# A depthwise conv on VectorE feeding a two-layer MLP on TensorE: taps issued across the chunks in turn, and four blocks in halves instead of nine

## Chip, cores, metric

One core of one Trainium2 chip. The metric is the time of one execution on the device in microseconds (us), the median of several runs. A profile is one execution of its own; its span is some 1.7 us shorter than the time.

## The reference, cut to what matters

```python
# x [8, 4096, 192], weight [8 heads, 7 taps]; softmax over the taps, then a causal conv per channel
out = np.einsum('hk,bskhg->bshg', softmax(weight), x_unfolded)
# 32768 tokens: 192 -> 2048 -> 192
h = x @ w_in
g = np.maximum(0.01 * h, h)
return g @ w_out
```

## The kernel before

A block is 512 positions of two batch rows, 32 blocks in all. Three chunks of 64 channels lie beside one another in a block's conv tile `y`; the two batch rows share the 128 partitions. VectorE does the conv of the next block while TensorE does the two layers of this one. The first nine blocks go in two halves of 256 positions, each a "group" of its own:

```python
NHALF = 9
groups = [(b, h * HT, HT) for b in range(NHALF) for h in range(2)]
groups += [(b, 0, ST) for b in range(NHALF, NBLK)]

def conv_jobs(grp, chunks=range(NCH)):            # NCH = 3 chunks, K = 7 taps
    ...
    for c in chunks:
        for k in range(K):
            ...
            if k == 0:
                jobs.append(... nc.vector.tensor_scalar_mul(d, s, wk[:, c, 0:1]))
            else:                                  # d = s * wk + d
                jobs.append(... nc.vector.scalar_tensor_tensor(
                    out=d, in0=s, scalar=wk[:, c, k:k+1], in1=d, op0=mult, op1=add))
```

A step of TensorE is a part of the first layer (`mm1`: 12 matmuls of 512 columns, or 24 of 256 in a half; on 64 rows each) and then 16 slots of the second layer (`mm2`: 32 matmuls of 192 columns). A whole block has eight steps, a half four. A whole block's second layer can only begin when its first is complete, so at the passage from halves to whole blocks a plan cuts the second layer short for a while:

```python
plan = {
    2 * NHALF - 2: [16, 8, 8, 16],
    2 * NHALF - 1: [8, 8, 16, 16],
    2 * NHALF: [16, 8, 8, 16, 8, 8, 16, 16],
}
...
copy = nc.scalar.copy if b < NHALF else nc.vector.tensor_copy     # eviction of the second layer
```

Of the kernel before, what the change touches and what calls it, by code (L numbers as in the profile page):

```python
# [14 lines left out]
def kernel(  # L15
# [11 lines left out]
    H, K = weight.shape  # L27
# [13 lines left out]
    NFC = F // 128  # L41
    NB = S // ST
    NBLK = (B // 2) * NB
    NHALF = 9
    RUN = 4
    NPEC = 2

# [14 lines left out]

    groups = [(b, h * HT, HT) for b in range(NHALF) for h in range(2)]
    groups += [(b, 0, ST) for b in range(NHALF, NBLK)]

# [107 lines left out]
    def conv_jobs(grp, chunks=range(NCH)):  # L173
        blk, t0, T = grp
        rp, st = divmod(blk, NB)
        if blk not in yt:
            yt[blk] = yt_pool.tile([128, NCH, ST], BF16, name="yt")
        y = yt[blk]
        jobs = []
        for c in chunks:  # L180
            for k in range(K):
                a = BASE + k + st * ST + t0
                src = xt[rp][:, c, a : a + T]
                dst = y[:, c, t0 : t0 + T]
                if k == 0:
                    jobs.append(
                        lambda s=src, d=dst, c=c: nc.vector.tensor_scalar_mul(  # L187
                            d, s, wk[:, c, 0:1]
                        )
                    )  # L190
                else:
                    jobs.append(
                        lambda s=src, d=dst, c=c, k=k: nc.vector.scalar_tensor_tensor(  # L193
                            out=d, in0=s, scalar=wk[:, c, k : k + 1], in1=d,
                            op0=mybir.AluOpType.mult, op1=mybir.AluOpType.add,
                        )
                    )
        return jobs
# [176 lines left out]
    for job in conv_jobs(groups[0], range(NPEC, NCH)):  # L375
        job()
# [92 lines left out]
    def evac_o(n):  # L469
# [4 lines left out]
        o_sb = osb[n // 2]  # L474
        copy = nc.scalar.copy if b < NHALF else nc.vector.tensor_copy
        ins = copy(out=o_sb[:, n % 2, :], in_=po.pop(n))  # L476
# [16 lines left out]
# [5 lines that stand above are left out]
    slot, avail = 0, 0  # L498
    for i, grp in enumerate(groups):
# [6 lines left out]
        if i == 0:  # L506
            ahead = []
        else:
            ahead = conv_jobs(groups[i + 1]) if i + 1 < len(groups) else []
        per = -(-len(ahead) // steps)  # L510
        for j in range(steps):
            for u in range(2 * j, 2 * j + 2):
                mm1(grp, u)
                if i == 0 and u == 1:
                    transpose_first(1)
                    evac_first(1, nc.vector.tensor_copy, nc.vector.tensor_copy)
                    pe_ahead, evac_y = pe_conv_jobs(groups[1], 0)
                    ahead = conv_jobs(groups[1], range(1, NCH))
                    per = len(ahead)
                if i == 0 and u == 3:  # L520

                    for job in pe_ahead:
                        job()
                    evac_y(act_scale)
                if i == 0 and u == 6:
                    transpose_first(2)
# [64 lines left out]
```

## Time and profile before

| | before |
|---|---|
| time, median of 3 runs | 692.91 us (692.07 to 692.96) |
| TensorE busy, profile | 684.0 of 690.9 us |
| VectorE busy, profile | 550.1 us |
| period of a step, halves / whole blocks | 2.630 / 2.615 us |

The prediction shows and reads the lines of this profile. One pair more is VectorE's accumulating taps by shape. Columns: line, engine, operation, names, shapes, count | busy us, mean ns of one | idle us before.

```profile
L193 DVE SCALAR_TENSOR_TENSOR yt<-xt,wk,yt 128x512 bf16<-128x512 bf16 x414 | 310.0, 749 | 10.2
L193 DVE SCALAR_TENSOR_TENSOR yt<-xt,wk,yt 128x256 bf16<-128x256 bf16 x306 | 148.4, 485 | 10.9
```

Busy time is 749 and 485 ns times the count: within a row nothing overlaps, and small gaps add up to 10 us in each.

### The profile page before, as it was taken

The numbers are of one execution on the slowest core, as the hardware profiler recorded it, in microseconds if no ns is written. First come the engines' busy times: TensorE is split into PE (matmuls) and PEld (weight loads), VectorE is DVE, ScalarE is ACT, GpSimd is POOL, SyncE is SP. The second block draws the span as 40 slices with busy tenths as digits, with TensorE's granted clock in tenths as the row PEclk, the third lists the DMA queues.
The fourth block names the chain that finished last, engine by engine and source line by source line (L and its number), as shares of the span: only waits on it lengthen the run. The fifth ranks groups of instructions, "written<-read, shape, count | busy, mean of one in ns | idle before, by whom it ended". The sixth has DMA issues, their size and how long they took to land.

```text
span 690.9 us, 26980 instructions
## 1 busy us (share of the span) xinstructions
PE 684.0 (99%) x12188; PEld 599.2 (87%) x12188; DVE 550.1 (80%) x1051; ACT 527.0 (76%) x609; POOL 147.1 (21%) x206
## 2 busy tenths in 40 slices
PE   8999999999999999999999999999999999999998
PEld 6999999999988888888888888888888888888887
DVE  6999999999986787878787878877878878787812
ACT  6888888888898777777777777777777777777771
POOL 7822220222222202222102222102222112000000
PEclk9999999999999999999999999999999999999999
DMA  9976454556649445566445565445664455322112
GB/s 153 117 92 94 76 79 82 68 75 83 82 71 94 72 81 74 67 93 82 67 84 68 75 83 87 74 74 76 77 82 74 81 73 70 67 60 59 47 42 65
DMA packets 184163, 53.85 MB, mean 78 GB/s; under 512 B 149104, under 2 KB 183664, under 8 KB 184048
## 3 DMA queue, kind: packets, MB, share of 16 engines
q0 software_dynamic: 99536, 14.76, 30.2%
q1 hardware_dynamic: 84512, 37.38, 22.8%
q8 instruction: 95, 1.56, 1.0%
q14 instruction: 20, 0.16, 0.1%
HBM read 29.88 MB, written 25.17 MB: 80 GB/s over the span
## 4 chain that ended last, share of the span: by engine, by line
PE 96%; ACT 1%; DMA 1%; POOL 1%; issue 0%; DVE 0%; POOLq 0%
PE po L429 49%; PE ph L403 47%; ACT g L410 1%; DMA w_in<-in_moe_w_in_dram 1%; POOL w_in L249 0%; POOL x_rows L123 0%; POOL sel L234 0%; DVE o_sb L476 0%; PE ptr L156 0%; POOL ident masks.py:199 0%; POOL sel L232 0%; POOL ident masks.py:197 0%; PE ptr L149 0%; POOLq masks.py:199 0%; POOLq L575 0%
## 5 line engine op out<-in xcount | busy, mean ns | idle before, releaser
L410 ACT ACTIVATE g<-ph 128x1024 bf16<-128x1024 f32 x512 | 496.2, 1021 | 143.2 <-PE ph L403 142.7
L193 DVE SCALAR_TENSOR_TENSOR yt<-xt,wk,yt 128x512 bf16<-128x512 bf16 (+1 forms) x720 | 458.3, 637 | 21.1
L429 PE MATMUL po<-w_out,g 64*128 64x192 bf16 (+1 forms) x8064 | 387.7, 243 | 0.0
L403 PE MATMUL ph<-yt,w_in 64*128 64x512 bf16 (+1 forms) x3936 | 384.7, 329 | 1.3 <-ACT g L410 0.7
L429 PEld LDWEIGHTS <-g 64*128 64x128 bf16 (+1 forms) x8064 | 360.5, 94 | 28.8 <-issue 0.2
L403 PEld LDWEIGHTS <-w_in 64*128 64x128 bf16 x3936 | 245.0, 111 | 54.6 <-issue 3.5
L78 POOL DMA_DIRECT2D x_bf<-in_x_dram x180 | 133.7, 777 | 424.6 <-DMA xt<-x_bf 422.0
L476 DVE COPY o_sb<-po 128x192 f32<-128x192 f32 x184 | 65.6, 357 | 109.1 <-PE po L429 100.4
L187 DVE TENSOR_SCALAR yt<-xt,wk 128x512 bf16<-128x512 bf16 (+1 forms) x120 | 40.6, 338 | 1.7 <-DMA xt<-x_bf 1.5
L476 ACT COPY o_sb<-po 128x192 f32<-128x192 f32 x72 | 23.0, 319 | 3.9 <-PE po L429 0.2
L284 PE MATMUL warm<-zero 128*128 128x256 bf16 (+1 forms) x20 | 4.5, 384 | 1.1 <-DVE junk L229 1.1
L212 PE MATMUL acc<-xt,diag 64*64 64x256 bf16 x84 | 5.0, 269 | 0.2 <-ACT xt L168 0.2
L168 DVE COPY xt<-ptr 128x384 bf16<-128x384 bf16 x7 | 2.2, 351 | 3.6 <-PE ptr L156 3.6
L212 PEld LDWEIGHTS <-diag 64*64 64x64 bf16 x84 | 4.5, 106 | 0.6 <-DVE xt L168 0.3
L127 POOL DMA_DIRECT2D x_half<-in_x_dram x6 | 4.3, 717 | 3.0 <-DMA w_in<-in_moe_w_in_dram 3.0
L284 PEld LDWEIGHTS <-zero 128*128 128x128 bf16 x20 | 2.4, 132 | 2.0 <-DVE junk L229 1.1
L249 POOL DMA_DIRECT2D w_in<-in_moe_w_in_dram x6 | 3.9, 656 | 0.0
L345 ACT ACTIVATE diag<-ident,whm 128x64 bf16<-128x64 bf16 x14 | 3.5, 335 | 0.0
L123 POOL DMA_DIRECT2D x_rows<-in_x_dram x4 | 2.9, 736 | 0.0
L156 PE MATMUL ptr<-ident,x_rows 64*64 64x64 bf16 x48 | 1.0, 196 | 1.3 <-DMA x_rows<-in_x_dram 1.3
L156 PEld LDWEIGHTS <-x_rows 64*64 64x64 bf16 x48 | 0.6, 108 | 1.9 <-DMA x_rows<-in_x_dram 1.7
L371 ACT ACTIVATE yt<-acc,rsum 128x256 bf16<-128x256 f32 x3 | 1.4, 467 | 1.0 <-PE acc L212 1.0
(37 smaller groups left out, 12.6 us busy)
## 6 DMA issues: line engine op xcount, KB each, us to landing
out_dram<-o_sb SPq DMA_DIRECT2D x117, 192.0 KB, 2.1
x_bf<-in_x_dram POOLq DMA_DIRECT2D x180, 64.0 KB, 3.3
out_dram<-o_sb SPq DMA_DIRECT2D x22, 96.0 KB, 1.6
xt<-x_bf SPq DMA_TRANSPOSE x90, 2.5
w_in<-in_moe_w_in_dram POOLq DMA_DIRECT2D x4, 192.0 KB, 5.6
w_in<-in_moe_w_in_dram POOLq DMA_DIRECT2D x2, 384.0 KB, 9.1
w_out<-in_moe_w_out_dram POOLq DMA_DIRECT2D x1, 768.0 KB, 11.2
x_nat<-in_x_dram SPq DMA_DIRECT2D x2, 192.0 KB, 2.6
```

The lines of the kernel that those rows point to most:

```text
L78: nc.gpsimd.dma_start(out=t[:, c, :, e, :], in_=src[2 * rp + e, :, :, c * CH : (c + 1) * CH],)
L127: nc.gpsimd.dma_start(out=x_half[q][:, c, :, e, :], in_=rows[:, e, :, c * CH : (c + 1) * CH],)
L187: lambda s=src, d=dst, c=c: nc.vector.tensor_scalar_mul(d, s, wk[:, c, 0:1])
L193: lambda s=src, d=dst, c=c, k=k: nc.vector.scalar_tensor_tensor(out=d, in0=s, scalar=wk[:, c, k : k + 1], in1=d, op0=mybir.AluOpType.mult, ...
L212: lambda k=k, p=p, a=a, e=e, ps=ps: nc.tensor.matmul(out=acc[ps, :T], lhsT=diag[c][ps, p, k, :], rhs=xt[0][ps, c, a : a + T], start=(k == ...
L249: nc.gpsimd.dma_start(out=w_in[n][e * CH : (e + 1) * CH], in_=moe_w_in[:, fs].rearrange("(c p) f -> p c f", p=CH),)
L284: nc.tensor.matmul(out=wa[:, 0, 0:cols], lhsT=zero[:, 0:128], rhs=zero[:, 0:cols], start=True, stop=True,)
L345: nc.scalar.activation(out=diag[c][:, p, k, :], in_=ident2, func=mybir.ActivationFunctionType.Copy, scale=whm[:, c, p, k : k + 1],)
L403: nc.tensor.matmul(out=ph[:, e, i * T : (i + 1) * T], lhsT=w_in_of(f, ps, c), rhs=y[ps, c, t0 : t0 + T], start=(c == 0), stop=(c == NCH - 1),)
L410: act = nc.scalar.activation(out=g[blk][:, nf * u : nf * (u + 1), :, t0 : t0 + T], in_=ph.rearrange("p e (i t) -> p i e t", i=nf), func=my ...
L429: return nc.tensor.matmul(out=po[m], lhsT=g[b][ps, fc, e, s * 128 : (s + 1) * 128], rhs=w_out[ps, fc, :], start=start, stop=stop,)
L476: ins = copy(out=o_sb[:, n % 2, :], in_=po.pop(n))
```

## The change

Each tap reads the accumulator that the tap before it wrote; such taps start 0.52 us apart in a half in the profile before, 35 ns more than one takes. Going through the chunks in turn, three accumulators alternate, and a tap need not wait for its neighbour: in the same profile, where a chunk ends, the next one's first tap starts 83 ns before the last tap's end. With a faster conv, fewer blocks should need to go in halves, and whole blocks need half the first-layer instructions.

```diff
-    NHALF = 9
+    NHALF = 4
...
-        for c in chunks:
-            for k in range(K):
+        for k in range(K):
+            for c in chunks:
```

## The prediction

> **What bounds the kernel now.** I read the page first: busy time by engine, the 40 slices, the chain that ended last, the waits; then the timeline of TensorE in one stretch with half blocks and one with whole blocks; last the timeline of VectorE.
>
> ```profile
> span 690.9 us, 26980 instructions
> PE 684.0 (99%) x12188; PEld 599.2 (87%) x12188; DVE 550.1 (80%) x1051; ACT 527.0 (76%) x609; POOL 147.1 (21%) x206
> PE   8999999999999999999999999999999999999998
> DVE  6999999999986787878787878877878878787812
> PE 96%; ACT 1%; DMA 1%; POOL 1%; issue 0%; DVE 0%; POOLq 0%
> ```
>
> TensorE is busy 684 of 690.9 us and is 96% of the chain that ended last. The listed waits of its matmuls come to 1.3+1.1+0.7+0.3+0.2 = 3.6 us, all in the start-up (input data, ScalarE's results), and none is for a conv result of VectorE. VectorE is close to full only in the first 12 slices or so, the nine blocks that go in halves.
>
> A busy TensorE may still not be at its peak, so I took the period of a step (the first-layer matmuls and then 32 second-layer ones):
>
> ```profile
> 102.88 1.51 PE L403 MATMUL ph<-yt,w_in 64*128 64x256 bf16 x24
> 104.19 1.52 PE L429 MATMUL po<-w_out,g 64*128 64x192 bf16 x32
> 105.51 1.51 PE L403 MATMUL ph<-yt,w_in 64*128 64x256 bf16 x24
> ...
> 300.55 1.49 PE L403 MATMUL ph<-yt,w_in 64*128 64x512 bf16 x12
> 301.85 1.52 PE L429 MATMUL po<-w_out,g 64*128 64x192 bf16 x32
> 303.17 1.49 PE L403 MATMUL ph<-yt,w_in 64*128 64x512 bf16 x12
> ```
>
> The first column is the start in us. With halves a step starts every 105.51-102.88 = **2.63 us**; with whole blocks it takes 2.62 here, and 2.615 as the mean of 168 steps between 216.79 and 656.11 us. A whole block needs half as many first-layer matmuls, yet its step is only 0.015 us shorter.
>
> [...]
>
> **The change, part by part.**
>
> *Order of the taps.* No instruction is added or removed; only VectorE's order changes. Now seven taps of one chunk follow one another, each reading the accumulator that the one before wrote:
>
> ```profile
> 102.33 0.34 DVE L187 TENSOR_SCALAR yt<-xt,wk 128x256 bf16<-128x256 bf16 x1
> 102.71 3.09 DVE L193 SCALAR_TENSOR_TENSOR yt<-xt,wk,yt 128x256 bf16<-128x256 bf16 x6
> 105.72 0.28 DVE L187 TENSOR_SCALAR yt<-xt,wk 128x256 bf16<-128x256 bf16 x1
> ```
>
> Six dependent taps take 3.09 us, 0.52 us each at a mean duration of 485 ns, so there are 35 ns of gap. The next chunk's first tap is independent and starts at 105.72, while the sixth ends only at 102.71+3.09 = 105.80: an overlap of 83 ns (median of such pairs). So an independent neighbour saves 35+83 = 118 ns. After the change nearly all of them are independent: I expect one tap to start 485-83 = 402 ns after the other in a half, and 749-83 = 666 ns in a whole block (now 785). One half's conv: 18x0.402 + 3x(0.300-0.083) = 7.9 us in place of 10.0; a whole block's: 18x0.666 + 3x(0.366-0.083) = 12.8 in place of 15.05. VectorE's busy time should fall from 550 to about 490 us. **None of this is on the path that sets the end**, for TensorE does not wait for the conv. Direct gain: 0.
>
> *Four blocks in halves, not nine.* Blocks 4 to 8 go whole. Per block 96 matmuls and 96 weight loads go, 480 of each; 5 x 21 conv instructions go; 40 evictions of 192 columns go from ScalarE (319 ns) to VectorE (357 ns). On TensorE: 5 blocks x 8 steps x (2.630-2.615) = **0.6 us** saved. The ScalarE and VectorE parts lie beside TensorE.
>
> *The passage from halves to whole blocks* moves from block 9 to 4 with the same plan of quotas. In it TensorE is held up in four steps of 8 quotas (2.22 us in place of 1.97), some 1 us in all, in either kernel. No difference.
>
> *Why halves at all.* VectorE's conv of a first whole block (15.05 us) is longer than the half (10.5 us) that hides it, so VectorE needs a lead. I computed it for each group as TensorE's first use minus the end of the last tap: 0 us for group 2, growing by 0.5 us per half, 6.4 us at group 16, and for block 9, the first whole one:
>
> ```profile
> 192.88 4.69 DVE L193 SCALAR_TENSOR_TENSOR yt<-xt,wk,yt 128x512 bf16<-128x512 bf16 x6
> ...
> 198.06 0.81 PE L403 MATMUL ph<-yt,w_in 64*128 64x512 bf16 x5
> ```
>
> The last tap ends at 197.57, TensorE starts at 198.06: nine was about the fewest that sufficed. With the new order a half gains 10.52-7.9 = 2.6 us of lead. In a hand count VectorE does group 1 by 20 us, waits for TensorE's transposes (31 us) before group 3, for transposed input before group 4 (about 42), then runs to group 7 by about 71 us, waits for block 4's transposes (issued in the middle of group 5, landed about 75) and finishes block 4 at about 75+12.8 = 88 us. TensorE reaches it at about 92.8 (group 6 starts at 73.87, then two shortened groups of 9.45 each). Lead: **some 4 to 5 us, no stall**. In the whole-block stage a step's work on VectorE is at most 3x0.666+0.36 = 2.4 us per 2.615, so it keeps pace.
>
> *Sum:* 692.9 - 0 - 0.6 = 692.3 us. The three runs before go from 692.07 to 692.96, so I put **692.2 us**.
>
> **Rivals.**
>
> *A: four halves give too little lead, because the interleaving brings less than 118 ns.* If it brought nothing, lead before group 8 would be the 2.5 us of now, the shortened groups cost 2x1.07 and the whole conv 5.0 more: -2.5-2.1 = about 4.7 us of stall at the first whole block, once, since from there on a block gives 20.9 us for 15. Time: 692.9+4.7-0.6 = 697. Against it: the 83 ns overlap is in every one of the chunk borders.
>
> *B: weight loads bound TensorE in the half stage* (their row shows 100% busy in halves, 83% in whole blocks), and removing them pays 17% of 105 us = 17 us, to 675. Against it: the measured periods differ by 0.6%[...]. Busy loads here lie under the matmuls.
>
> *C: with interleaving all three chunks finish together, late.* Today chunks 0 and 1 are done long before TensorE turns to a block. If the last tap of chunk 0 came after TensorE's first matmul, each of 28 blocks would wait a little: 0.3 us each would be 8 us, to 700. Against it: now in the steady stage the last tap ends 0.29 us after TensorE's first weight load of the block, harmless as it belongs to chunk 2. The three last taps in the new order end about 0.24 us earlier, and chunk 0's is the first of them, some 1.3 us ahead of need.
>
> *D: the transposes or loads of input, now issued earlier in blocks 4 to 8, or evictions on VectorE, hold TensorE.* The same order runs in 23 whole blocks without a wait. Near 0.
>
> **Range and chances.** A, C at the sizes above stay inside 2% (13.9 us), so only B or something not seen leaves it. The range is the 0.9 us spread of the runs before plus the uncertainty of 0.6 and a little room for a small stall: 691.3 to 693.3. Within 2%: 0.97; faster 0.02; slower 0.01.
>
> **What would show it.** Right: step period 2.615 us from about 93 us on; TensorE still 98 to 99% busy and without waits for the conv; first-layer matmuls 3456 in place of 3936; VectorE about 490 us busy, taps 0.40 and 0.67 us apart, idle more, waiting for transposes early and for second-layer results later; ScalarE about 514 us; block 4 finished on VectorE several us before TensorE's first 512-column matmul. Wrong: a gap on TensorE before that matmul (A), a period under 2.6 (B), a gap at every block's start (C).

That a busy TensorE may not be at its peak is to be seen in e2: busy 1.00 at a granted clock of 0.50.

## The result, and the profile after

| | before | after |
|---|---|---|
| time, median of 4 runs each | 692.93 us (692.07 to 693.41) | 692.50 us (692.28 to 692.71) |
| VectorE busy, profile | 550.1 us | 501.6 us |
| ScalarE busy, profile | 527.0 us | 514.4 us |
| group 1 to block 31, profile | 635.67 us | 635.06 us |

The ratio of after to before is 0.9992 (95% interval 0.9978 to 1.0006). A ratio here is the mean time of one kernel's runs over that of the other's of the same rounds, so not quite the ratio of the medians. A second set, five rounds on another occasion, gave 0.9987 (0.9974 to 1.0000).

From the page after:

```profile
span 690.8 us, 25914 instructions
PE 685.2 (99%) x11708; PEld 584.0 (85%) x11708; DVE 501.6 (73%) x986; ACT 514.4 (74%) x569; POOL 148.0 (21%) x206
PE   9999999999999999999999999999999999999998
DVE  5899666777777787777787777777777877777712
```

VectorE lost 48.5 us of work and is above nine tenths in two slices only, not in the first twelve. TensorE stayed at 99%: the freed time became idle time of VectorE. The same two shapes by form:

```profile
L193 DVE SCALAR_TENSOR_TENSOR yt<-xt,wk,yt 128x512 bf16<-128x512 bf16 x504 | 348.5, 744 | 0.0
L193 DVE SCALAR_TENSOR_TENSOR yt<-xt,wk,yt 128x256 bf16<-128x256 bf16 x126 | 51.0, 478 | 0.2
```

One tap still takes 744 or 478 ns, but busy time is now less than count times mean (504 x 0.744 = 375 us against 348.5): they overlap. The idle 10 us before them are gone. The timeline of VectorE around the first whole block (start us, length us):

```profile
65.14 0.67 DVE L187 TENSOR_SCALAR yt<-xt,wk 128x256 bf16<-128x256 bf16 x3
65.73 7.21 DVE L193 SCALAR_TENSOR_TENSOR yt<-xt,wk,yt 128x256 bf16<-128x256 bf16 x18
75.84 0.35 DVE L187 TENSOR_SCALAR yt<-xt,wk 128x512 bf16<-128x512 bf16 x1 [2.90 <-DMA xt<-x_bf]
76.85 0.35 DVE L187 TENSOR_SCALAR yt<-xt,wk 128x512 bf16<-128x512 bf16 x1 [0.66 <-DMA xt<-x_bf]
79.05 0.35 DVE L187 TENSOR_SCALAR yt<-xt,wk 128x512 bf16<-128x512 bf16 x1 [1.85 <-DMA xt<-x_bf]
79.32 12.01 DVE L193 SCALAR_TENSOR_TENSOR yt<-xt,wk,yt 128x512 bf16<-128x512 bf16 x18
```

18 taps in 7.21 us with a last one of 0.48 are (7.21-0.48)/17 = 0.396 us apart; in the whole block (12.01-0.74)/17 = 0.663. In the kernel before it was 0.52 and 0.79 within a chunk (medians). The order has a price too: the first taps of all three chunks come first, so VectorE now waits for all three transposes, which land at about 75.8, 76.8 and 79.0 us, where the old order could have begun on chunk 0 alone. In all, VectorE's taps wait 12.6 us for transposes in this profile, 1.5 us in that of the kernel before.

TensorE at the first whole block and in the steady stage:

```profile
92.00 1.52 PE L429 MATMUL po<-w_out,g 64*128 64x192 bf16 x32
93.33 1.50 PE L403 MATMUL ph<-yt,w_in 64*128 64x512 bf16 x12
...
300.42 1.49 PE L403 MATMUL ph<-yt,w_in 64*128 64x512 bf16 x12
301.72 1.52 PE L429 MATMUL po<-w_out,g 64*128 64x192 bf16 x32
303.04 1.49 PE L403 MATMUL ph<-yt,w_in 64*128 64x512 bf16 x12
```

No wait is noted at the first whole block: the conv ended at 91.33 and TensorE's first matmul on it starts at 93.33. The steady period is 303.04-300.42 = 2.62 as before.

**Why the stretch and not the span.** The spans differ by 0.1 us, though 0.6 us was saved. The rest went at the start, in which neither profile notes a wait of TensorE for VectorE's conv. Here are the 56 conv matmuls that TensorE itself does for the first group, before and then after:

```profile
6.33 3.26 PE L212 MATMUL acc<-xt,diag 64*64 64x256 bf16 x56 [0.17 <-ACT xt L168]
```

```profile
6.56 4.95 PE L212 MATMUL acc<-xt,diag 64*64 64x256 bf16 x56
```

The same work took 1.7 us longer. The trace's first record of full clock begins 5.4 us after the start in the kernel before and 10.1 us in this profile. Of the 1.7 us only 0.48 are left where group 1 begins, since the kernel before then waits 1.00 and 0.31 us for input (the DMA of `x_rows`) and the changed one, being later, does not. Over the ten profiles full clock begins anywhere between 5.4 and 10.3 us, and group 1 between 20.4 and 22.2 us. The clock is not the only thing that scatters: in e6 it was full from 7.3 us on, and group 1 still began latest of all, after a wait of 1.20 us for the DMA of `w_in`.

What sets the start of full clock is not shown; the ten starts spread over 4.9 us. The lengths are less scattered: every record of full clock in the ten profiles lasts, to 0.05 us, a whole number of 3.413 us (13, 26, 175, 187, 200 or 201 of them; 686.08 us in the kernel before, 682.67 in this profile), and 3.413 us is the length of the record of half clock in e2.

So I compare the stretch from the first `mm1` weight load of group 1 to that of block 31 (20.44 to 656.11 us before, 20.92 to 655.98 after, found by counting the loads in the trace): 635.67-635.06 = **0.61 us** saved. A timeline shows nearly the same stretch, from the first second-layer step to block 31's first matmul, before and then after:

```profile
22.48 1.52 PE L429 MATMUL po<-w_out,g 64*128 64x192 bf16 x32
...
656.19 1.49 PE L403 MATMUL ph<-yt,w_in 64*128 64x512 bf16 x12
```

```profile
22.96 1.52 PE L429 MATMUL po<-w_out,g 64*128 64x192 bf16 x32
...
656.06 1.49 PE L403 MATMUL ph<-yt,w_in 64*128 64x512 bf16 x12
```

That is 633.71 and 633.10 us, again 0.61 apart.

### The profile page after: what moved, and what is told of

The parts are those of the page before. It is cut to its first block, busy times and chain, and to the rows that moved or that the text cites. A ratio compares the mean times of both kernels' runs of the same rounds, so it can differ in the third digit from the quotient of the medians.

```text
span 690.8 us, 25914 instructions
## 1 busy us (share of the span) xinstructions
PE 685.2 (99%) x11708; PEld 584.0 (85%) x11708; DVE 501.6 (73%) x986; ACT 514.4 (74%) x569; POOL 148.0 (21%) x206
## 4 chain that ended last, share of the span: by engine, by line
PE 98%; ACT 2%; issue 0%; DVE 0%
PE po L429 49%; PE ph L403 47%; ACT g L410 2%; PE acc L212 1%; PE warm L284 1%; PE ptr L149 0%; ACT yt L371 0%; DVE o_sb L476 0%; PE ptr L156 0%; PE wps L320 0%; PE wps_l L320 0%; DVE zero L227 0%; DVE junk L229 0%
## 5 line engine op out<-in xcount | busy, mean ns | idle before, releaser
L193 DVE SCALAR_TENSOR_TENSOR yt<-xt,wk,yt 128x512 bf16<-128x512 bf16 (+1 forms) x630 | 399.5, 691 | 0.2
L403 PEld LDWEIGHTS <-w_in 64*128 64x128 bf16 x3456 | 226.0, 111 | 64.7 <-issue 3.7
L476 DVE COPY o_sb<-po 128x192 f32<-128x192 f32 x224 | 80.1, 358 | 163.9 <-PE po L429 156.3
L187 DVE TENSOR_SCALAR yt<-xt,wk 128x512 bf16<-128x512 bf16 (+1 forms) x105 | 36.8, 381 | 12.8 <-DMA xt<-x_bf 12.6
L476 ACT COPY o_sb<-po 128x192 f32<-128x192 f32 x32 | 10.2, 320 | 1.5 <-PE po L429 0.2
L212 PE MATMUL acc<-xt,diag 64*64 64x256 bf16 x84 | 6.7, 327 | 0.0
```

Source lines behind the costliest of these rows:

```text
L187: lambda s=src, d=dst, c=c: nc.vector.tensor_scalar_mul(d, s, wk[:, c, 0:1])
L193: lambda s=src, d=dst, c=c, k=k: nc.vector.scalar_tensor_tensor(out=d, in0=s, scalar=wk[:, c, k : k + 1], in1=d, op0=mybir.AluOpType.mult, ...
L212: lambda k=k, p=p, a=a, e=e, ps=ps: nc.tensor.matmul(out=acc[ps, :T], lhsT=diag[c][ps, p, k, :], rhs=xt[0][ps, c, a : a + T], start=(k == ...
L403: nc.tensor.matmul(out=ph[:, e, i * T : (i + 1) * T], lhsT=w_in_of(f, ps, c), rhs=y[ps, c, t0 : t0 + T], start=(c == 0), stop=(c == NCH - 1),)
L476: ins = copy(out=o_sb[:, n % 2, :], in_=po.pop(n))
```

## The experiments

Theory: TensorE alone sets the time. The order of the taps is worth nothing by itself; halves exist only to give VectorE a lead; the saving is 0.015 us per step that no longer goes in halves. Rivals: the order itself acts on the path; halves are not needed at all; weight loads bound the stage with halves; the profile's period is an artefact.

The stretch from group 1 to block 31, read from each profile as above, is free of the start-up's scatter:

| kernel | order | halved blocks | time, median us | ratio to before (95%) | stretch us |
|---|---|---|---|---|---|
| before | by chunk | 9 | 693.16 / 693.48 | 1 | 635.67 |
| changed | in turn | 4 | 692.50 | 0.9992 (0.9978 to 1.0006) | 635.06 |
| e8, changed again | in turn | 4 | 692.40 | 0.9987 (0.9974 to 1.0000) | 635.05 |
| e1 | in turn | 9 | 693.31 | 1.0002 (0.9985 to 1.0019) | 635.71 |
| e2 | by chunk | 4 | 698.84 | 1.0081 (1.0066 to 1.0096) | 640.92 |
| e3 | in turn | 2 | 697.25 | 1.0057 (1.0041 to 1.0073) | 639.26 |
| e4 | in turn | 24 | 695.77 | 1.0036 (1.0021 to 1.0051) | 637.46 |
| e5 | in turn | 3 | 693.12 | 0.9997 (0.9983 to 1.0011) | 634.94 |
| e6 | in turn, chunks reversed | 4 | 692.68 | 0.9990 (0.9977 to 1.0003) | 635.59 |
| e7 | in turn, evictions moved | 3 | 692.78 | 0.9989 (0.9977 to 1.0002) | 634.94 |

The two medians of before are those of the two sets of runs (e1 to e4 on one chip, e5 to e8 on another); the set of the row "changed" had 692.93. A stretch is read from one profile, but it repeats well: 635.06 and 635.05 for the changed kernel, 634.94 twice for three halves. All outputs were correct.

### e1: the order alone

```diff
-    NHALF = 4
+    NHALF = 9
```

(against the changed kernel)

> Only the order of the taps is changed, nine blocks stay in halves. Theory (TensorE bounds, VectorE's conv lies beside it): time as before, 692.9 us, ratio 1.000 within 0.001; step periods 2.63 and 2.615 us unchanged; VectorE busy about 505 us instead of 550, taps of a half 0.40 us apart; lead of the conv at the first whole block (block 9) several us instead of 0.4. Rival (the order itself is on the path, through chunks that finish late or through the gain of VectorE): a change of more than 2 us, or a gap on TensorE at the start of every block.

The stretch is 635.71 us, 0.04 from before. The page:

```profile
PE 686.1 (99%) x12188; PEld 600.1 (87%) x12188; DVE 502.0 (73%) x1051; ACT 527.1 (76%) x609; POOL 147.6 (21%) x206
```

Its 502.0 us for VectorE against 550.1 are the whole fall of the changed kernel, and they bought nothing. TensorE has no wait for the conv anywhere. The lead at block 9 is 2.3 us (VectorE ends at 196.56, TensorE starts at 198.84), less than the "several us" expected: in the half stage it was up to 12.3 us, but then VectorE waited 3.05 us for a free `y` buffer and 2.56 us for transposes just before that block. The theory stands; the order alone is worth 0.

### e2: fewer halves alone

```diff
-        for k in range(K):
-            for c in chunks:
+        for c in chunks:
+            for k in range(K):
```

(against the changed kernel)

> Only the number of half blocks is changed (four), the taps stay chunk after chunk. Theory (halves are there to give VectorE a lead): VectorE finishes block 4 at about 82.2+15.05 = 97.2 us, TensorE gets there at about 93 and needs chunk 2 some 0.4 us later, so one stall of about 4 us before block 4 on TensorE waiting for the conv, none later; 0.6 us saved by the shorter steps; about 696.3 us, ratio to before about 1.005. Rival (four halves would have been enough in the old order too, the old nine was only habit): about 692.3 us and no wait.

The stall is there and as long as expected. TensorE's timeline at block 4:

```profile
93.89 0.63 PE L403 MATMUL ph<-yt,w_in 64*128 64x512 bf16 x4
98.57 1.90 PE L403 MATMUL ph<-yt,w_in 64*128 64x512 bf16 x8 [4.05 <-DVE yt L193]
100.23 2.33 PE L429 MATMUL po<-w_out,g 64*128 64x192 bf16 x32
```

Four matmuls use chunks 0 and 1, then TensorE waits 4.05 us for chunk 2, whose conv ends at 98.52. But the kernel is 5.86 us slower than the changed one in the stretch, not 4. The next lines show why: 32 second-layer matmuls take 2.33 us where they take 1.52 elsewhere. The windows of this profile (after the length, the busy times of PE, PEld, DVE, ACT and POOL; then the granted clock, and two numbers on DMA):

```profile
98.00:99.00 1.00, 0.43 (x4) 0.19 (x5) 0.96 (x3) 0.00 (x0) 0.67 (x1) 0.76 0.00 0
99.00:100.00 1.00, 1.00 (x8) 0.51 (x6) 0.96 (x2) 0.77 (x1) 1.00 (x3) 0.50 0.18 12
100.00:101.00 1.00, 1.00 (x14) 0.76 (x10) 0.96 (x2) 0.74 (x2) 1.00 (x2) 0.50 1.21 77
101.00:102.00 1.00, 1.00 (x18) 1.00 (x16) 0.93 (x3) 0.54 (x1) 1.00 (x2) 0.53 1.53 97
102.00:103.00 1.00, 1.00 (x20) 0.78 (x17) 0.96 (x2) 0.32 (x1) 0.80 (x2) 1.00 1.25 79
```

After the stall TensorE ran at half clock for 3.413 us (one record in the trace, from 98.53 us on), which costs half of that, 1.71 us. 4.05+1.71 = 5.76 of the 5.86 us. The theory's mechanism holds; its sum missed the clock.

### e3: two halves

```diff
-    NHALF = 4
+    NHALF = 2
```

> The changed kernel with two blocks in halves instead of four. Theory: the conv of block 2, the first whole one, starts at about 40 us when its transposes land and takes 14 us with the waits for the three of them, so ends at about 54; TensorE gets there at about 51.2: a stall of 2 to 3 us, less 0.24 us saved: about 694.9 us, 2.4 over the changed kernel. Rival (with the interleaved order VectorE is fast enough without lead, so that no halves are needed): about 692.3 us and no wait for the conv.

```profile
48.52 1.51 PE L403 MATMUL ph<-yt,w_in 64*128 64x256 bf16 x24
...
53.30 0.41 PE L403 MATMUL ph<-yt,w_in 64*128 64x512 bf16 x2 [1.95 <-DVE yt L193]
53.96 0.50 PE L403 MATMUL ph<-yt,w_in 64*128 64x512 bf16 x2 [0.25 <-DVE yt L193]
54.62 1.90 PE L403 MATMUL ph<-yt,w_in 64*128 64x512 bf16 x8 [0.16 <-DVE yt L193]
...
58.23 1.47 PE L403 MATMUL ph<-yt,w_in 64*128 64x512 bf16 x12
```

The waits are 1.95+0.25+0.16 = 2.36 us, in the range expected, one for each chunk because the three now finish 0.66 us apart. Again a record of 3.413 us at half clock follows, so 2.36+1.71-0.24 = 3.8 of the 4.20 us over the changed kernel. A wait is counted from the modelled end of the last matmul, and that leaves 0.4 us out. By starts nothing is missing: the two steps take 53.30-48.52 = 4.78 and 58.23-53.30 = 4.93 us in place of 2.630 and 2.615, together 4.46 too long, less 0.24 is 4.22. Two of the four runs, 697.87 and 698.37 us, had a mean clock of 0.995, the profiled one (696.64) and the fourth 0.998; a second record of half clock would fit, but no trace of those two was kept. Halves are needed with the new order too, for two blocks are too few.

### e4: 24 halves

```diff
-    NHALF = 4
+    NHALF = 24
```

> The changed kernel with 24 blocks in halves instead of four, to enlarge the cost of a half. Theory (a step with halves costs 2.630 instead of 2.615 us on TensorE): 20 blocks x 8 x 0.015 = 2.4 us more than the changed kernel, about 694.9 us, ratio to before 1.0026. Rival (weight loads, busy 100% in halves, bound that stage): the half stage would cost much more than 0.6% and 20 blocks would add 10 us or more. Second rival (the difference of the periods is an artefact of the profiled run): 692.5 us.

The stretch is 637.46-635.06 = 2.40 us longer than that of the changed kernel: 20 blocks at 0.12 us, to the digit. Weight loads busy 94% of the whole span (654.4 us on its page) don't bound it. That the difference of the periods is no artefact of the profile is not shown by the stretch, which is read from a profile too, but by the time: 1.0036 of before (1.0021 to 1.0051), where 1.0026 was expected and an artefact would have left the changed kernel's 0.999.

### e5: three halves

```diff
-    NHALF = 4
+    NHALF = 3
```

> The changed kernel with three blocks in halves. Two halved blocks stalled TensorE (waits of 2.4 us and then 3.4 us at half clock). Theory: the conv of block 3 starts at about 57 us in VectorE's order, with 12.8 us of taps and perhaps 2.5 us for transposes that land apart ends at 70 to 72; TensorE gets there at 72.2: no wait or one of under 0.5 us, and no half clock; 692.4 us, the same as with four. Rival (the lead is short here as well): a wait of 1 us or more, then the half clock, 695 us.

There is no wait at block 3 and no half clock there: VectorE ended at 70.89 us, TensorE's first matmul on the block starts at 72.96. The stretch is 0.12 us shorter than with four, as one block fewer in halves should give. The time doesn't tell them apart.

### e6: the chunks of a tap in reverse

```diff
-            for c in chunks:
+            for c in reversed(chunks):
```

> The changed kernel with the three chunks of each tap in reverse order, so that chunk 0, which TensorE needs first, is finished last, 0.04 us after TensorE's first weight load of the block where the profile of the changed kernel has the last tap. Theory (the order of the chunks inside a tap matters, since the last taps of a block end just in time): TensorE waits some 0.05 to 0.15 us at the start of each of 26 whole blocks: 1.3 to 4 us more than the changed kernel, 694 to 696 us, visible as a step of 2.7 us once per block. Rival (there is slack that the profile does not show): 692.5 us, no longer step.

The step at each block's border did get longer, but by less than expected: by the starts of TensorE's matmuls over the last 20 blocks it has 2.6325 us, all seven others 2.6150 us, which all eight have in the changed kernel. That is 17.5 ns x 26 blocks = 0.46 us; the stretch is 0.53 us longer, 0.46 us if it is taken between matmuls instead of weight loads. In the three blocks looked at the first weight load starts 0.05 us after the end of chunk 0's last tap; in the changed kernel it starts 0.04 us before the last tap, then chunk 2's, ends. So the concern behind rival C was real, but its size is tens of ns and not the 50 to 150 expected: the last taps do end just in time, and the order inside a tap counts a little.

### e7: evictions moved off ScalarE at the passage

```diff
-        copy = nc.scalar.copy if b < NHALF else nc.vector.tensor_copy
+        copy = nc.scalar.copy if (b, s) < (NHALF - 1, HS) else nc.vector.tensor_copy
```

(against e5)

> Three blocks in halves, and the evictions of the second half of the last halved block go to VectorE instead of ScalarE, which is what TensorE waits for in the four steps of 8 quotas. Theory: in the two such pairs of the first whole block ScalarE then does only its activations, 4 x 1.02 = 4.08 us per pair instead of 4.4, so the pair takes about 4.1 us on TensorE instead of 4.2: 0.2 us saved in all, not to be told from e5 by the clock but in the profile. Rival: the evictions hold up VectorE's conv of the next block and TensorE waits for it.

A miss: the stretch is 634.94 us, as in e5, and the pair of short steps still takes 1.96+2.22 us. ScalarE's timeline in this profile shows that the eviction was not between the activations that TensorE is held up by:

```profile
75.54 3.89 ACT L410 ACTIVATE g<-ph 128x1024 bf16<-128x1024 f32 x4 [0.33 <-PE ph L403]
79.33 0.32 ACT L476 COPY o_sb<-po 128x192 f32<-128x192 f32 x1
```

Four activations follow one another without a gap, with evictions only outside. In e5, where nothing was moved, it is the same: four activations from 76.46 us for 3.89 us, the eviction after them at 80.25. So the edit had nothing to take away there, and the experiment says nothing of what an eviction between them would cost. With two buffers for their input, that chain alone can account for the 0.25 us; that last step is argued, not tested.

### e8: the changed kernel again

> The changed kernel once more, beside the others, for a narrower interval and a second profile. Theory: 0.6 us less than before in the stretch from the first matmul of group 1 to that of block 31; in the whole time 0 to 1 us less, ratio 0.998 to 1.000. In the first profile TensorE's record of full clock began 10.1 us after the start, in that of the kernel before 5.4 us; if this is chance, it may fall anywhere between about 5 and 10 us here.

The stretch is 635.05 us (first profile 635.06). The median is 692.40 us, from 691.86 to 693.98; full clock began at 7.5 us this time.

## Why the prediction was right, point by point

**Time and the sum: right.** 692.2 was said, 692.5 measured, within 691.3 to 693.3. The only term, 40 steps x 0.015 = 0.6 us, measured 0.61 us in the stretch, and e4 confirmed it at four times the size. That the median itself came so near is partly luck: before's own median was 692.93, 693.16 and 693.48 us in its three sets, a scatter as large as the gain, and the interval of the time includes no change. Where the 15 ns come from was not said there, and can be read from the trace of the kernel before: the pairs of matmuls start 215.85, 109.14 and 82.50 ns apart at 512, 256 and 192 columns (means over the stage with whole blocks and that with halves). Two pairs of 256 columns take 218.28 ns, 2.43 more than one of 512, and six times that is 15 ns. The sums are 6 x 215.85 + 16 x 82.50 = 2615 ns and 12 x 109.14 + 16 x 82.50 = 2630 ns, the two periods, so a step holds no wait besides these spacings. That a pair could not start sooner is not shown.

**"None of this is on the path": right,** e1 shows it. The tap intervals were right as well (0.402 and 0.666 said, 0.396 and 0.663 measured). VectorE's busy time was mis-sized: 490 said, 501.6 measured. A 512-column tap takes 348.5/504 = 0.691 us of it, not 0.666, which is 13 us over 504 taps. In the steady stage each batch of two or three taps ends before an eviction that waits for TensorE, so its last tap is followed by nothing and shows its full length: 8 batches x 83 ns x 26 blocks = 17 us at most that the sum took as overlapped (an estimate from these profiles).

**"Some 4 to 5 us, no stall": no stall was right, the lead was not.** The end of block 4's conv was put at 75+12.8 = 88 us; it was 91.33, the lead 2.0 us (1.5 in e8). The failed term is the landing of the input: the prediction let all three chunks land at about 75, but they were waited for 2.90, 0.66 and 1.85 us, the last tap of the first round starting at 79.05. Interleaving shortens the conv (12.8 us for the whole block in e5, 15.05 before), but its first round has to wait for the chunk that lands last.

**Rival A** was rightly discarded. Its stall, about 4.7 us (the sum printed as -2.5-2.1 is the lead of 2.5, less 5.0 for the conv, less 2.1), was right: in e2 the conv ends 98.52-93.89 = 4.63 us after TensorE's first matmul on the block. But its time, 697, was too low: e2 has 698.84. The step missing was the 3.413 us at half clock after the stall, 1.71 us in e2. **Rival B** fell with e4 (17% of 105 us is 18, as its 675 has it, not 17). **Rival C** is real at 17.5 ns per block when provoked (e6), not at the 0.3 us that was set beside it. **Rival D** showed nothing: the periods from block 6 on are the same.

**What the prediction did not foresee** is that the start-up scatters by more than the whole gain (20.4 to 22.2 us until group 1), so the spans of one profile of each kernel would have shown 0.1 instead of 0.6 us.

## What to carry to other kernels

Before making an engine faster, ask whether the bounding engine waits for it: here 48 us of VectorE's time were won and 0 us of the kernel's. What such a gain can do is make another arrangement possible (fewer halves), and then only that arrangement's own saving counts, so work it out from the periods of the bounding engine. When an effect is smaller than the start-up's scatter, compare a stretch that excludes the start, and enlarge the suspected cost (24 halves) until it stands clear.
